# One core, linear attention beside a state-space convolution: another order, other places, banks and copy engines for the same operations

## The chip, the core and the metric

The kernel runs on one core of a Trainium2 chip. The core has a matrix engine (PE, with its weight loads PEld), a vector engine (DVE), a scalar engine (ACT), a general engine (POOL) and a sync engine (SP), which here issues nearly all transfers. Each engine takes its own instructions strictly in the order in which the program lists them; engines wait for each other through semaphores. The metric is the device time of one execution in microseconds. Three executions of the kernel before took 239.25, 239.59 and 239.7 us: median 239.59.

## The reference

Two independent blocks share the call, and their outputs are laid side by side. All inputs are bf16.

```python
# block A: linear attention, S = 2048 rows, D = 448, 16 heads of 28
qkv = x @ wqkv                              # split into q, k, v by head
phi_q = [softmax(q @ w_phi), softmax(-q @ w_phi)]
phi_k = [softmax(k @ w_phi), softmax(-k @ w_phi)]
kv, z = phi_k.T @ v, sum(phi_k)
a = (phi_q @ kv / (phi_q @ z + 1e-6)) @ wo
# block B: a diagonal state-space model, L = 2048, D = 448, N = 256 states
K[d, l] = Re( sum_n C[d,n] * dt[d] * B[d,n] * exp(dt[d] * A[d,n] * l) )
b = causal_convolution(u, K) + u * Dskip    # in the reference by FFT
out = concatenate([a, b], axis=-1)
```

## The kernel before

**The work.** Block A is done in `key_side` (eight pairs of row tiles: projections on PE, exponentials on ACT, a transposing transfer of the exponentials, sums, reciprocals and products on DVE) and in four calls of `query_side` (512 rows each). Its weights are folded first: `fold_weights` multiplies W_phi into W_q and W_k. Block B first brings A, B and C into a layout by states (`to_states`), computes powers of the complex pole (exponentials for the size, sines for the angle), and then for each of four groups of channels builds tables (`rotations`, `dampings`, `damp`, `far`, `hi_tables`), sums them on PE to the kernel K (`build_k`), scatters it through DRAM (`scatter_k`), takes its spectrum by matrix products (`kernel_spectrum`), multiplies spectra on DVE and transforms back (`conv`). The spectrum of u is made once, in `signal_spectrum(0)` and `signal_spectrum(1)`.

**The order.** Nothing is issued while the functions run. Each step calls `prog.add` and becomes an operation with a running number (0 to 1035) and an engine; one operation is a single instruction, save on PE, where it is a group of matmuls. At the end `prog.run(ORDER)` issues the operations in the order of a list of numbers. So the list alone decides in which order each engine's queue stands. Three more lists are read as the steps are recorded: `PLACES` gives each buffer its byte offset in SBUF (buffers may share a place one after the other), `SLOTS` gives each PE group its bank or pair of banks of PSUM (eight banks, 0 to 7), and `PICKS` gives each of 210 copies, scalings and squares its engine, A for ACT or V for DVE. A step that writes to a place or bank waits until the reader of what was there is done. The tile framework adds these waits.

**Operations that the text names by number.**

| number | engine | what it is (line) |
|---|---|---|
| 0, 3 | SP, ACT | load of log_dt (275); load of A_re, issued from ACT's queue (280) |
| 5, 7, 9, 6, 8 | SP | loads of A_im, B_re, B_im, C_re, C_im (285) |
| 10 to 25 | SP | 16 transposing loads of x (287), 14 to 17 the second 512 rows |
| 26, 28, 31 to 34 | SP | loads of W_qk, of most of W_V, of W_phi in four blocks (291, 293, 298) |
| 41, 42, 43 | ACT, DVE, either | exp of log_dt, DG, and DGN = -DG (305 to 309) |
| 44, 49 | PE | A_re and A_im to states (333) |
| 45 to 48, 50 to 53 | either, DVE | their copies and differences (337, 338) |
| 54 to 57 | DVE | products of C and B (342) |
| 58 to 62 | ACT | five exponentials, 128, 16, 8, 32 and 64 times the log of the pole's size (353) |
| 63, 65; 64, 66 | PE; either | the products to states (356) and their copies (357) |
| 70, 71; 74, 75; 77, 78; 80, 81; 83, 84 | ACT | cosine and sine for 128; 16; 8; 32; 64 (366, 367) |
| 72, 76, 79, 82, 85 | DVE | size times angle for 128, 16, 8, 32, 64 (368) |
| 86 to 88 | either, DVE | the square of the power 128 (372 to 374) |
| 104, 106; 105, 107; 108, 109 | PE; either; DVE | first block of u: reversal of its rows in two halves, the copies, sum and difference (411 to 415) |
| 139, 141; 140, 142; 143, 144 | PE; either; DVE | the same for the second block of u |
| 95, 116, 119, 126 | PE, either, SP, either | a transposition of weights (391), a copy of the signal's spectrum (429), a store of it (431), another such copy |
| 167, 168 | DVE | the diagonal of Dskip, in two parts (443) |
| 196 | PE | arguments of the first dampings (461) |
| 294 | PE | a key projection, on the second 512 rows of x (601) |

**The start before.** ORDER begins 3 0 41 1 2 42, so the load of A_re is the first entry of ACT's queue and the load of log_dt the first of SP's. The groups 104, 106, 139 and 65 follow each other in banks 4 and 5, 63 and 141 in 0 and 1, and 196 has 6 and 7.

## Time and profile before

| | |
|---|---|
| median of three executions | 239.59 us |
| the profiled execution | 239.25 us, span 237.4 us from first to last instruction |
| busy: PE / DVE / ACT / POOL | 210.4 / 220.2 / 186.5 / 4.9 us |
| table loads of ACT | 10, 1.28 us each |
| bytes moved | 36.40 MB, mean 153 GB/s |
| mean granted clock of PE | 0.984 |

In a line of the profile, L220 is line 220 of the kernel. As most steps go through small helpers (177 tensor-tensor on DVE, 198 activations, 205 copies, 220 groups of matmuls), the line tells the helper and not the place; shapes and times tell which step it is. "Idle before, releaser" is the time in which an engine did nothing before an instruction, and whose semaphore ended it. PE's busy time has modelled ends. The granted clock is the share of PE's clock that a throttle let through.

### The profile page before, as it was taken

What the parts mean: (1) busy time and instruction counts of PE and PEld (TensorE: products, weight loads), DVE (VectorE), ACT (ScalarE), POOL (GpSimd) and SP (SyncE); (2) the same over time, 40 slices, a digit from 0 to 9 for tenths busy, and PEclk for the clock granted to TensorE, in tenths of its full rate; (3) what the DMA queues carried; (4) which work ended last, traced back from release to release, by engine and by line L of the source; (5) the groups of instructions that cost most, each with busy time, mean ns of one, the idle gap of its engine ahead of it and who ended that gap; (6) DMA issues with size and microseconds to landing.
All of it is one profiled execution on the core that took longest, in us unless ns stands there. A gap on an engine that the chain in (4) does not pass through costs nothing. (4 is left out here: it accounts for less than half of the span.)

```text
span 237.4 us, 7131 instructions
## 1 busy us (share of the span) xinstructions
PE 210.4 (89%) x3044; PEld 152.8 (64%) x3044; DVE 220.2 (93%) x294; ACT 186.5 (79%) x324; POOL 4.9 (2%) x20
## 2 busy tenths in 40 slices
PE   1156989999998998989899999979999999999994
PEld 1143446555466665669677579755579958589993
DVE  1999999999999998989999999979999999999991
ACT  2999999999999999899999999972648545335420
POOL 2000001000000100000000000000000000000000
PEclk9995899999999999999999999999999999999999
DMA  6999944930399039989457265943689697583454
GB/s 160 243 214 260 207 113 100 275 125 3 99 213 252 7 77 175 172 155 239 128 148 161 18 124 116 277 150 95 52 254 274 134 184 240 82 178 119 70 143 98
DMA packets 81640, 36.40 MB, mean 153 GB/s; under 512 B 65480, under 2 KB 79688, under 8 KB 81224
## 3 DMA queue, kind: packets, MB, share of 16 engines
q1 hardware_dynamic: 81368, 35.71, 67.8%
q8 instruction: 24, 0.39, 0.7%
q10 hardware_dynamic: 240, 0.23, 0.3%
q14 instruction: 8, 0.07, 0.1%
HBM read 19.44 MB, written 8.62 MB: 118 GB/s over the span
## 5 line engine op out<-in xcount | busy, mean ns | idle before, releaser
L220 PE MATMUL psum<-sbuf 128*128 128x112 bf16 (+9 forms) x3000 | 208.3, 251 | 23.4 <-DVE sbuf L177 10.5
L177 DVE TENSOR_TENSOR sbuf<-sbuf 128x896 bf16<-128x896 bf16 (+13 forms) x240 | 198.9, 895 | 8.3 <-ACT sbuf L198 4.7
L220 PEld LDWEIGHTS <-sbuf 128*128 128x128 bf16 (+3 forms) x3000 | 150.2, 114 | 80.0 <-issue 18.6
L205 ACT CAST sbuf<-psum 128x448 bf16<-128x448 f32 (+4 forms) x128 | 82.2, 710 | 34.0 <-PE psum L220 33.7
L198 ACT ACTIVATE sbuf<-psum 128x448 bf16<-128x448 f32 (+4 forms) x110 | 65.6, 683 | 2.4 <-PE psum L220 2.3
L211 ACT ACTIVATE sbuf<-sbuf 128x896 bf16<-128x896 bf16 (+1 forms) x19 | 15.0, 836 | 2.8 <-DVE sbuf L177 2.7
L198 ACT ACT_TABLE_LOAD x10 | 12.8, 1283 | 1.4 <-PEq L901 1.2
L198 ACT ACTIVATE sbuf<-psum,sbuf 128x896 f32<-128x896 f32 (+3 forms) x17 | 13.5, 817 | 0.0
L208 ACT ACTIVATE sbuf<-sbuf 128x896 bf16<-128x896 bf16 (+3 forms) x11 | 9.9, 898 | 3.8 <-DVE sbuf L177 3.8
L205 ACT COPY sbuf<-psum 112x896 bf16<-112x896 bf16 (+2 forms) x12 | 7.2, 645 | 2.2 <-PE psum L230 2.2
L205 DVE CAST sbuf<-psum 128x448 bf16<-128x448 f32 (+2 forms) x9 | 6.0, 680 | 2.4 <-PE psum L220 1.3
L215 POOL MEMSET sbuf<- 128x224 bf16 (+4 forms) x15 | 4.5, 323 | 153.4 <-PE psum L220 118.7
L205 ACT COPY sbuf<-sbuf 128x224 bf16<-128x224 bf16 (+3 forms) x15 | 6.3, 453 | 0.0
L194 DVE RECIPROCAL sbuf<-psum 128x64 bf16<-128x64 f32 x8 | 4.3, 546 | 2.0 <-PE psum L220 1.4
L177 DVE TENSOR_TENSOR sbuf<-psum,sbuf 128x448 bf16<-128x448 f32 (+3 forms) x12 | 4.9, 440 | 0.0
L230 PE MATMUL psum<-sbuf 112*112 112x112 bf16 (+1 forms) x44 | 3.7, 216 | 0.2 <-ACT sbuf L198 0.2
L230 PEld LDWEIGHTS <-sbuf 112*112 112x112 bf16 (+1 forms) x44 | 3.1, 128 | 1.0 <-DVE sbuf L177 0.3
L212 DVE TENSOR_TENSOR sbuf<-sbuf 128x1792 f32<-128x1792 f32 (+1 forms) x2 | 2.6, 1318 | 0.0
L208 DVE TENSOR_SCALAR sbuf<-sbuf 128x1568 bf16<-128x1568 bf16 (+2 forms) x5 | 2.3, 456 | 0.0
L194 DVE RECIPROCAL sbuf<-sbuf 128x64 f32<-128x64 f32 x4 | 2.2, 543 | 0.0
L189 DVE SCALAR_TENSOR_TENSOR sbuf<-sbuf 128x64 f32<-128x64 f32 (+1 forms) x5 | 1.9, 389 | 0.0
L205 ACT CAST sbuf<-sbuf 128x1792 bf16<-128x1792 f32 x1 | 1.7, 1718 | 0.0
(10 smaller groups left out, 3.9 us busy)
## 6 DMA issues: line engine op xcount, KB each, us to landing
SUd<-sbuf SPq DMA_DIRECT2D x8, 448.0 KB, 4.6
sbuf<-SCd SPq DMA_DIRECT2D x16, 224.0 KB
sbuf<-SUd SPq DMA_DIRECT2D x4, 896.0 KB
sbuf<-const SPq DMA_DIRECT2D x3, 1024.0 KB
sbuf<-const SPq DMA_DIRECT2D x8, 384.0 KB, 5.0
sbuf<-in_B_u_dram SPq DMA_DIRECT2D x4, 448.0 KB, 7.5
out_dram<-sbuf SPq DMA_DIRECT2D x4, 448.0 KB, 2.8
out_dram<-sbuf SPq DMA_DIRECT2D x16, 112.0 KB, 3.1
```

What stands on the lines that cost most here:

```text
L177: prog.add("V", lambda: nc.vector.tensor_tensor(out=o, in0=a, in1=b, op=op))
L189: prog.add("V", lambda: nc.vector.scalar_tensor_tensor(out=o, in0=a, scalar=s, in1=b, op0=op0, op1=op1))
L194: nc.vector.reciprocal(o, a)
L198: prog.add("A", lambda: nc.scalar.activation(o, a, fn, **kw))
L205: either(lambda: nc.scalar.copy(o, a), lambda: nc.vector.tensor_copy(o, a))
L208: either(lambda: nc.scalar.activation(o, a, ACT.Copy, scale=s), lambda: nc.vector.tensor_scalar_mul(o, a, s))
L211: either(lambda: nc.scalar.activation(o, a, ACT.Square), lambda: nc.vector.tensor_tensor(out=o, in0=a, in1=a, op=ALU.mult))
L212: lambda: nc.vector.tensor_tensor(out=o, in0=a, in1=a, op=ALU.mult))
L215: prog.add("G", lambda: nc.gpsimd.memset(o, v))
L220: nc.tensor.matmul(o, lhsT=l, rhs=r, **kw)
L230: nc.tensor.transpose(o, i, idn)
```

## The change

The functions stay as they are, and so do all operations and their shapes. ORDER, PLACES, SLOTS and PICKS are replaced by other lists. The load of A_re (3) is still the first entry of ACT's queue and log_dt (0) the first of SP's. Then SP has 8, 5, 7, 9, 6 and PID, where it had 5, 7, 6, 9, 8 and PID. The groups 65, 106, 141 and 139 now follow each other in banks 4 and 5, and 63, 104 and 196 in banks 6 and 7. The load 28 moves from the middle of the loads of x to a place ahead of all of them. 22 of the 210 entries of PICKS differ: 43, 138, 161, 384, 429, 865, 937, 1000, 1004, 1018 and 1034 go from DVE to ACT; 208, 210, 215, 514, 625, 654, 656, 797, 828, 879 and 882 go from ACT to DVE. (1000 and 1004 are copies of the last kernel spectrum; 1018 and 1034 are copies of the last output tiles.)

```diff
 ORDER = [int(i) for i in (
-    "3 0 41 1 2 42 43 44 35 5 49 7 60 58 62 6 45 9 27 8 67 50 52 4 51 53 71 54 70 46 37 81 77 78 56 47 38 80 57 30 "
-    "65 31 48 66 61 196 33 104 105 59 72 106 40 55 201 202 107 63 199 39 36 86 88 200 87 16 139 64 140 29 79 82 18 "
-    "141 142 108 112 17 109 143 25 198 13 197 90 205 83 160 162 26 161 84 34 75 172 163 92 178 74 91 144 113 89 165 "
-    "122 85 176 76 175 125 174 155 126 207 171 177 173 179 206 10 208 209 95 123 68 180 120 19 127 20 212 156 97 96 "
-    "69 121 211 210 110 130 128 164 11 32 98 402 132 384 111 131 133 381 145 22 99 214 101 213 100 216 21 103 404 "
-    "215 15 115 403 24 217 181 14 219 182 183 116 28 405 147 12 102 146 117 185 184 148 290 73 218 118 152 187 221 "
-    "220 186 293 124 406 134 204 136 222 94 135 137 294 223 274 114 188 170 264 279 224 226 138 129 153 225 150 276 "
...
-    "789 1006 1024 1017 989 758 1025 1026 1027 754 986 1029 1011 761 987 976 977 990 1020 1021 1033 1028 1018 1030 "
-    "777 1022 973 974 1019 1034 1035 1031 1032 "
+    "1 2 67 3 0 41 42 43 8 44 5 49 60 59 7 9 35 50 58 52 51 53 61 55 70 30 57 47 6 54 71 80 4 56 48 81 65 39 63 37 "
+    "72 74 45 66 82 46 86 38 78 88 106 83 64 104 40 107 141 77 75 87 79 105 196 142 36 139 84 109 108 140 122 62 "
+    "143 120 144 123 202 199 200 172 76 90 85 92 160 121 89 201 28 198 91 15 31 197 112 210 19 161 402 179 208 180 "
+    "17 204 125 175 205 177 68 12 69 117 178 176 33 181 113 26 404 94 183 127 174 126 34 173 95 206 118 403 97 98 "
+    "10 23 207 115 130 18 116 209 182 212 132 128 184 211 13 110 131 155 73 185 214 96 213 186 32 406 215 187 147 "
+    "119 133 29 16 217 162 111 156 216 148 188 101 103 99 189 405 203 163 124 11 102 150 14 27 165 20 218 136 21 "
+    "100 151 134 407 135 138 294 164 114 304 306 137 219 408 22 384 221 296 220 297 145 146 190 264 259 171 222 149 "
+    "157 307 191 335 409 262 24 170 289 410 152 223 267 224 225 261 193 226 228 266 153 192 279 227 291 292 93 412 "
...
+    "761 966 988 1013 1015 1017 1024 973 1025 774 613 614 989 1016 1018 990 976 987 974 1026 1027 1020 1029 1033 "
+    "1019 1021 1028 1030 961 1034 1035 1022 977 1031 1032 "
 PLACES = [64 * int(i) for i in (
-    "3536 13 4 3407 3408 2404 991 959 1071 2554 3280 778 2688 2194 435 2632 2540 935 2334 2348 1169 1522 2250 2586 "
...
+    "1554 3559 801 32 2259 2323 1399 2379 2291 2411 3303 968 1431 0 2868 1119 2564 266 37 51 507 2198 2291 0 2443 "
...
 SLOTS = [[int(c) for c in i] for i in (
-    "01 23 01 45 3 2 4 01 23 45 45 23 45 67 67 01 67 23 67 0 6 23 56 45 01 45 01 01 01 45 23 01 67 01 67 4 7 2 3 1 "
...
+    "01 23 67 45 2 6 7 23 01 67 45 01 45 01 23 45 23 67 45 2 7 01 67 45 45 01 45 45 12 23 67 23 67 01 67 1 4 0 2 6 "
...
 PICKS = (
-    "VAVVVAAAAVVAAAAAAAAAAAAAAAAAAAVAAAAAAAAVAVVAAAAVVAAVAAAAAAAAAAAAAAAAAAAAAVAAAAAVAVAVAAAAAAAAAAAAAAAA"
-    "AAAAAAAAAAAAAAAAAAAAAVAAAAAAAAAAAAAAAAAAAAAAAAAAAAAAAAAAAAAAAAAAAAAAAAAVAAAAAAAAAAAAAAAAVAAAAAAAAAAA"
-    "AAVAVAVAAV"
+    "AAVVVAAAAVVAAAAAAAAAAAAAAAAAAAAAAAAAAAAAAVVAVVVVVAAVAAAAAAAAAAAAAAAAAAAAAAAAAAAVAAAVAAAAAAAAAAAVAAAA"
+    "AAAAAAAAAAAAAAAAAAAAVVAVVAAAAAAAAAAAAAAAAAAAAAAAAAAAAAAVAAAVAAAAAAAAAAAAAAAVAVAAAAAAAAAAAAAAAAAAAAAA"
+    "AAAAAAAAAA"
```

## The prediction

> **What bounds the kernel now.** I read the engines' busy times first, then the granted clock by slice, then busy time in stretches of 12 us, then the first 30 us in order of time. Busy times and clock, from the page:

> ```profile
> PE 210.4 (89%) x3044; PEld 152.8 (64%) x3044; DVE 220.2 (93%) x294; ACT 186.5 (79%) x324; POOL 4.9 (2%) x20
> ...
> PEclk9995899999999999999999999999999999999999
> ```

> DVE has 237.4 - 220.2 = 17.2 us without work, PE 27. A new order can win no more than a part of that. Busy time by stretches (length, then us busy and count of PE, PEld, DVE, ACT, POOL; then granted clock, DMA share, GB/s):

> ```profile
> 36.00:48.00 12.00, 11.76 (x99) 7.41 (x98) 11.89 (x16) 11.95 (x19) 1.16 (x3) 1.00 0.74 195
> ...
> 144.00:156.00 12.00, 10.21 (x262) 8.62 (x259) 12.00 (x17) 11.97 (x23) 0.00 (x0) 1.00 0.86 189
> ...
> 216.00:228.00 12.00, 12.00 (x249) 12.00 (x246) 11.74 (x12) 6.24 (x13) 0.00 (x0) 1.00 0.53 120
> ```

> Up to 156 us DVE and ACT are both full, later DVE and PE. A wait on any full engine is passed on to the end, unless a later wait swallows it. Most of PE's idle time lies in the first 30 us, where it waits for copies that empty its banks; PE in order of time (start, us, what, idle before it and who ended that):

> ```profile
> 11.66 3.08 PE L220 MATMUL psum<-sbuf 112*128 112x112 bf16 x23 [0.86 <-DVE sbuf L177]
> 16.32 0.54 PE L220 MATMUL psum<-sbuf 128*128 128x448 bf16 x2 [1.58 <-ACT sbuf L205]
> 19.34 3.22 PE L220 MATMUL psum<-sbuf 128*128 128x448 bf16 x20 [2.49 <-ACT sbuf L205]
> 23.15 6.21 PE L220 MATMUL psum<-sbuf 128*128 128x448 bf16 x26 [0.58 <-ACT sbuf L205]
> 29.63 0.93 PE L220 MATMUL psum<-sbuf 128*128 128x224 bf16 x8 [0.28 <-DVE sbuf L205]
> ```

> ACT and DVE in the same stretch: ACT's start-to-start time is 0.89 for a cosine (12.75 to 13.64) and 0.80 for a sine (13.64 to 14.44), it loses only 0.18 us here, and DVE loses 0.50.

> ```profile
> 12.75 1.02 ACT L198 ACTIVATE sbuf<-psum,sbuf 128x896 f32<-128x896 f32 x1
> 13.64 0.94 ACT L198 ACTIVATE sbuf<-psum 128x896 f32<-128x896 f32 x1
> 14.44 1.04 ACT L198 ACTIVATE sbuf<-psum,sbuf 128x896 f32<-128x896 f32 x1
> ...
> 24.09 0.91 ACT L205 CAST sbuf<-psum 128x896 bf16<-128x896 f32 x1 [0.18 <-PE psum L220]
> ```

> ```profile
> 25.03 3.03 DVE L177 TENSOR_TENSOR sbuf<-sbuf 128x1792 bf16<-128x1792 bf16 x2 [0.50 <-ACT sbuf L205]
> ```

> The granted clock there, in stretches of 2 us:

> ```profile
> 16.00:18.00 2.00, 0.54 (x2) 0.19 (x2) 2.00 (x3) 1.97 (x3) 0.00 (x0) 1.00 1.15 227
> 18.00:20.00 2.00, 0.66 (x2) 0.25 (x2) 2.00 (x2) 2.00 (x4) 0.00 (x0) 0.53 0.93 379
> ...
> 22.00:24.00 2.00, 1.42 (x5) 0.39 (x4) 2.00 (x3) 1.91 (x3) 0.00 (x0) 0.50 0.96 154
> 24.00:26.00 2.00, 2.00 (x9) 0.86 (x8) 1.50 (x2) 1.91 (x3) 0.00 (x0) 0.76 0.91 272
> ```

> The clock is halved from about 18.1 to 24.95. A pair of 128x448 matmuls takes 0.54 at 16.32 and 0.90 at 19.34.

> **The change, part by part.**

> *A_re.* In both kernels it is the first instruction of ACT's queue, issued at 0.80 beside the first issue of SP; PE starts at 4.49 when it lands. It is not moved: 0. The number of table loads is 10 in both: 0.

> *Engines of copies.* 22 of 210 change sides, 11 each way. DVE loses 5.5 us by its own rows (1.07 for a 128x896 cast from PSUM, five casts of 448 columns from PSUM at 0.62, five small ones at 0.17 to 0.41, 1.35 together) and gains 3.7 (two strided 128x224 copies at 0.41, four of 448 columns at 0.27, one of 224 at 0.21, one from PSUM at 0.28, squares at 0.62 and 0.38, a scale at 0.28). Two of these rows, by shape (busy, mean ns, idle before):

> ```profile
> L205 DVE CAST sbuf<-psum 128x448 bf16<-128x448 f32 x7 | 4.3, 632 | 2.3 <-PE psum L220 1.3 <-issue 1.0
> ...
> L205 DVE COPY sbuf<-sbuf 128x448 bf16<-128x448 bf16 x3 | 0.8, 269 | 0.0
> ```

> Of what it loses, 2 x 0.62 is the pair of final copies, which stood behind DVE's last product and held up nothing: on the path -5.5 + 1.24 + 3.7 = **-0.6**. The copy of 128x128 from PSUM has no row on DVE; between 0.28 (a product of that size from PSUM) and 0.62 I take 0.28, which it resembles in size; the end 0.62 costs 0.3 more. ACT loses 6.4 and gains about 5.7.

> *SP's queue at the start.* C_im now goes ahead of A_im, which lands one 224 KB load later. The first 12 us move 201 GB/s, so 1.1 us later than before at about 4.9 plus a fixed delay like A_re's: about 5.7. PE's group on A_im started at 5.60 for other reasons: +0.1.

> *Banks and order of the first 26 us.* This is the largest term. Follow it by operation numbers. DVE after 42: 50, 52, 51, 53, 55, 57, 47, 54, 56, 48 from 6.65 at about 0.56 each, ending at 12.3, as long as before. ACT: 43 first (DG is ready at 4.84, so 4.88 to 5.43), then four exponentials from 5.84 at 0.81, to 9.2; table load 1.28, to 10.5. Then, at 0.89 a cosine, 0.80 a sine and 0.68 to 0.90 a copy: 70, 71, 80, 81, 74, 45, 66 (15.45 to 16.35), 78, 83, 64 (to 18.95), 107 (to 19.75), 77, 75, 105 (21.35 to 22.3), 142 (to 23.1), 84, and ACT is free for 140 at 23.75. PE works through two pairs of banks only: 63, 104 and 196 share 6 and 7; 65, 106, 141 and 139 share 4 and 5. So 104 waits for copy 64 (19.0), 141 for 107 (19.8), and 196 for 105: 22.3. In the kernel before 196 ran at 13.04, in banks that were free. PE's queue is in order, and 139 stands behind 196. At the halved clock 196 takes 1.70 (what it took before; the same eight 128x224 matmuls take 0.93 at 29.63 at full clock) and 139 0.95: 22.3 + 1.70 + 0.95 = 24.95. So copy 140 waits 1.2 on ACT and ends at 25.9, and DVE's 143 and all behind it wait for that. DVE, by the products before it (72 at 12.35, 82, 46, 86, 88, 87, 79 to 22.6, 109, 108), is free at 24.65: it waits **1.3**. DVE's waits up to 143 are then 4.22 + 1.75 + 0.05 + 1.3 = 7.3 against 4.22 + 1.33 + 0.50 = 6.05 before: **+1.25**. ACT's are 1.25 + 1.38 + 0.76 + 0.41 + 1.2 = 5.0 against 4.6: +0.4.

> [...]

> *SP's queue from 8 to 50 us.* The load of W_V (28) now stands ahead of all transposed loads of x and reuses a place that DVE's 79 reads, so SP stands still from about 8 to 22.6; before it waited to 14.15. Behind it are 16 transposes (1.26 us of issue each), W_qk and the W_phi blocks. W_qk issues at about 29.3 and lands by 35; its user, transposition 95, waits for copy 126 at 39: hidden. The last transpose that the first key product (294) needs is behind the store 119, which waits for ACT's 116 (43): 14 issues at about 47.5 and lands 3.9 later, 51.4; 294 is due at 53: hidden by 1.5 us. If SP is later than that by x, PE loses x - 1.5.

> *The body, 26 to 220 us.* I compared running sums of the rows: work of DVE before an operation against work of ACT or PE before its source. The furthest that ACT lags behind DVE is 2.8 us in the new order (near 145 us) and 1.8 in the old; the furthest that ACT lags behind PE is 2.6 against 2.9. With ACT's +0.4 neither passes what DVE and PE had really waited by then (time less work done: 9.6 and 19.6 us). I take the same waits as before, **+0.4** for ACT's own delay, which holds up PE's banks until 156 us; the ends are -2.7 and +2.0, from the rivals.

> *The tail.* The same operations in nearly the same order: DVE's last products, then two inverse groups of PE (3.71), a copy (0.53) and the last store. 168 joins DVE's last products: +0.2, beside PE's 12.00 of 12: 0.

> Sum: +1.25 - 0.6 + 0.4 = **+1.05**. The profiled execution took 239.25, the lowest of three with a median of 239.59: 240.3 against its own time, 240.6 against the median. I forecast **240.5**.

> **Rivals.**

> *Faster: the waits of the key side go.* In the old kernel PE waits three times for the transposed exponentials, near 74, 94 and 104 us (view of the waits: us, times, longest):

> ```profile
> PE psum L220 <- DMA sbuf<-sbuf: 2.7, 3, 1.2
> ```

> In the new order the first of those transposes issues at about 64 and lands at 68, while its matmul is due at 69.6; the others come out level. If all three go, the time is 240.5 - 2.7 = 237.8. Against it: ACT is full there, so PE may wait for ACT's copies in their place. It decides for faster from 1.6 us on, all that the sum above adds and the bound of measurement.

> [...]

> *Slower: SP late for x.* Single transposes took 1.78 (at 19.18) where most took 1.26. Seven in line before 14 at +0.5 are 3.5 us, 1.5 of that is covered: 242.5. The old order had its transposes spread from 14.6 on, the new one crowds them behind 22.6.

> **How the numbers follow.** Forecast 0.44, key side 0.25, full clock 0.11, SP late 0.20. About 0.2% (0.48 us) is what a measurement can tell from no change. The forecast's own range is 239.9 to 241.6, which puts 0.03 of it within 0.2%; of the full clock's 0.11, 0.08 is within and 0.03 below. Faster 0.28, same 0.11, slower 0.61. The range reaches to both rivals: 237.6 to 243.0.

> **What the profile after would show.** The clock at a half near 18 to 25 us; a group of eight 128x224 matmuls at about 22 with a wait on ACT before it; an ACT wait on PE of about 1.2 and a DVE wait on ACT of about 1.3 near 25 us; DVE busy 218.3; SP idle from about 8 to 22.6 and no PE wait on in_A_x near 53. If DVE's 143 starts before 25.3, the head term is wrong; if PE waits for sbuf<-sbuf go, the first rival holds; a PE wait on in_A_x or in_A_wqkv speaks for the last. I would be wrong altogether if the body's waits, which I carried over unchanged, came out otherwise by more than 2 us: running sums bound them from below alone.

## The result, and the profile after

The changed kernel takes 246.51 us (median of six, 245.81 to 247.36), the kernel before 239.42 us (six runs, 238.65 to 240.12) beside it: a ratio of 1.0301, 95% interval 1.0270 to 1.0333. It is 7.1 us slower. The forecast was 240.5 us and the range ended at 243.0, so the direction was right and the size far off. The profiled execution took 246.2 us and its span is 244.5, against 237.4 before. Single runs of a kernel can come out more than 1.5% above its fastest one; the ratios and intervals here leave such runs out, the medians do not.

The page of the changed kernel, busy times, granted clock and the chain that ended last:

```profile
PE 212.8 (87%) x3044; PEld 153.4 (63%) x3044; DVE 218.3 (89%) x294; ACT 185.6 (76%) x324; POOL 6.0 (2%) x20
...
PEclk9999999999999999999999999799999999899999
...
DVE 16%; PE 11%; DMA 5%; issue 1%; SPq 1%; ACT 1%; DVEq 0%
```

DVE is busy for 218.3 us, as forecast, 1.9 less than before, and yet the span is 7.1 longer: DVE's idle time went from 17.2 to 26.2. The row of the clock has two dips, near 157 and 208 us, that before does not have. It shows none in the head, but the trace holds no record of the clock there (see the head, below). Transfers now stand in the last chain with 5%. The view of the waits of the changed kernel (engine, what waited, for what: us in total, times, longest):

```profile
PE psum L220 <- issue: 4.8, 2, 2.5
...
DVE sbuf L177 <- DMA sbuf<-SUd: 4.6, 1, 4.6
...
DVE sbuf L194 <- ACT sbuf L205: 2.8, 1, 2.8
PE psum L220 <- DMA sbuf<-sbuf: 2.3, 2, 2.2
DVE sbuf L177 <- issue: 2.3, 1, 2.3
```

and the line of the kernel before that answers to the first of these:

```profile
PE psum L220 <- issue: 2.2, 2, 1.7
```

The last of these lines is DVE's wait at 159.26, behind the first of two stops of PE that are looked at below. The 2.8 us stand ahead of the reciprocal 286, at 74.67. There the kernel before waited 0.59 us, and the changed kernel in turn no longer has four waits of 0.45 to 0.78 us that DVE had between 81 and 120 us.

**The tail.** The 4.6 us are DVE's wait ahead of operation 1012, the first product of the last group of channels. DVE, PE and SP of the changed kernel in order of time (start, us, engine, line, what, and idle before it and who ended that):

```profile
224.48 12.68 DVE L177 TENSOR_TENSOR sbuf<-sbuf 128x3584 bf16<-128x3584 bf16 x13 [4.64 <-DMA sbuf<-SUd]
```

```profile
205.82 6.42 PE L220 MATMUL psum<-sbuf 128*32 128x80 bf16 x26 [2.47 <-issue]
```

```profile
209.39 3.43 SPq L240 DMA_DIRECT2D sbuf<-KTd  x6
216.30 1.54 SPq L240 DMA_DIRECT2D out_dram<-sbuf  x3
217.94 0.47 SPq L240 DMA_DIRECT2D sbuf<-SUd  x1
```

In the kernel before, 1012 began at 219.87 without a wait and its load (1007, 896 KB) had been issued at 209.81. Now the load stands in SP's queue behind the store 777, SP stands still for 3.48 us until 216.30, and the load lands at 224.4. But 1012 also needs ScalarE's copy 996 (end 223.53, before 216.63), which hangs on PE, and 777 waits for a copy of PE's results as well. So there are two readings. Either the order of SP's queue costs 4.6 us (the queue theory), or PE is late and drags both along.

**PE's stop.** PE is late because of the stop in the second of these three views: from 203.35 to 205.82 it does nothing, in the middle of group 889, and no semaphore holds it (the page calls that "issue"). In the kernel before such a stop lasted 0.46 us in the same place. What moves meanwhile, by DMA queue, in the stretch 198.5 to 203.0 of the changed kernel:

```profile
DMA packets 1426, 1.25 MB, mean 277 GB/s; under 512 B 1257, under 2 KB 1298, under 8 KB 1426
...
q1 hardware_dynamic: 1426, 1.25, 106.6%
```

and in the stretch 203 to 205:

```profile
DMA packets 86, 0.04 MB, mean 20 GB/s; under 512 B 84, under 2 KB 84, under 8 KB 84
...
q8 instruction: 1, 0.02, 4.5%
```

The queue q8 carries instructions, 24 packets of 16 KB in each kernel. Its packet starts at 203.06, lands at 204.49, and PE goes on at 205.82. Until 203 the DMA engines were full with the load of SU[2] (962, 896 KB, issued at 197.35), a store and two transposing loads. Counting PE's matmuls and weight loads in the trace (6088 in all), the stop is at number 5042; the other stop without a semaphore, 2.34 us from 153.47, is at 3508, and a packet of q8 had started at 153.55 there as well. With the entries for semaphores in PE's queue counted too (13 ahead of the one stop, 15 ahead of the other) the numbers are 5057 and 3521, the ones that the expectations use, and they are exactly 6 times 256 apart. Both stops lie in strips of `build_k`, where a group of ten small matmuls takes 0.3 us; from 149.74 to 153.47 PE issues 70 instructions per us, so 256 last 3.7 us. The kernel before has its two stops at 3507 and 5043, which with those entries are 3521 and 5057 as well. The fetch theory: PE runs out of instructions in these strips when the packet with the next 256 stands behind other transfers. With both stops of the changed kernel comes a half clock of 3.41 us (from 155.39, just before the first one ends, and from 206.59, just behind the second), with those of before none. By sums of busy time PE lost 1.6 us more than before in the first strip, and 4.5 against 0.5 in the second.

### The profile page after: what moved, and what is told of

Its sections match the earlier page's. It is cut to its first block, busy times and chain, and to the rows that moved or that the text cites. A ratio compares the mean times of both kernels' runs of the same rounds, so it can differ in the third digit from the quotient of the medians.

```text
span 244.5 us, 7117 instructions
## 1 busy us (share of the span) xinstructions
PE 212.8 (87%) x3044; PEld 153.4 (63%) x3044; DVE 218.3 (89%) x294; ACT 185.6 (76%) x324; POOL 6.0 (2%) x20
## 3 DMA queue, kind: packets, MB, share of 16 engines
q1 hardware_dynamic: 81368, 35.71, 68.3%
HBM read 19.44 MB, written 8.62 MB: 115 GB/s over the span
## 5 line engine op out<-in xcount | busy, mean ns | idle before, releaser
L220 PE MATMUL psum<-sbuf 128*128 128x112 bf16 (+9 forms) x3000 | 210.7, 252 | 27.6 <-ACT sbuf L205 7.0
L177 DVE TENSOR_TENSOR sbuf<-sbuf 128x896 bf16<-128x896 bf16 (+12 forms) x240 | 199.1, 894 | 13.4 <-DMA sbuf<-SUd 4.6
L220 PEld LDWEIGHTS <-sbuf 128*128 128x128 bf16 (+3 forms) x3000 | 150.8, 115 | 86.0 <-issue 22.7
L205 ACT CAST sbuf<-psum 128x448 bf16<-128x448 f32 (+4 forms) x134 | 85.5, 709 | 40.9 <-PE psum L220 38.8
L198 ACT ACTIVATE sbuf<-psum 128x448 bf16<-128x448 f32 (+4 forms) x110 | 65.6, 707 | 1.0 <-PE psum L220 0.9
L211 ACT ACTIVATE sbuf<-sbuf 128x896 bf16<-128x896 bf16 (+1 forms) x17 | 13.6, 877 | 9.9 <-DVE sbuf L177 9.7
L198 ACT ACTIVATE sbuf<-psum,sbuf 128x896 f32<-128x896 f32 (+3 forms) x17 | 13.5, 817 | 0.0
L208 ACT ACTIVATE sbuf<-sbuf 128x896 bf16<-128x896 bf16 (+4 forms) x11 | 10.0, 913 | 0.8 <-DVE sbuf L299 0.8
L215 POOL MEMSET sbuf<- 128x224 bf16 (+4 forms) x15 | 5.5, 404 | 153.3 <-PE psum L220 121.4
L205 ACT COPY sbuf<-psum 112x896 bf16<-112x896 bf16 (+2 forms) x12 | 7.1, 617 | 0.0
L177 DVE TENSOR_TENSOR sbuf<-psum,sbuf 128x448 bf16<-128x448 f32 (+3 forms) x12 | 5.1, 442 | 0.3 <-ACT sbuf L205 0.2
L205 ACT COPY sbuf<-sbuf 128x224 bf16<-128x224 bf16 (+2 forms) x11 | 4.0, 374 | 0.0
L205 DVE CAST sbuf<-psum 128x448 bf16<-128x448 f32 x3 | 1.8, 645 | 2.3 <-PE psum L220 2.3
L212 DVE TENSOR_TENSOR sbuf<-sbuf 128x896 bf16<-128x896 bf16 (+2 forms) x4 | 3.6, 908 | 0.0
L205 DVE COPY sbuf<-sbuf 128x448 bf16<-128x448 bf16 (+1 forms) x10 | 2.4, 265 | 0.0
```

What stands on the lines that cost most here:

```text
L177: prog.add("V", lambda: nc.vector.tensor_tensor(out=o, in0=a, in1=b, op=op))
L198: prog.add("A", lambda: nc.scalar.activation(o, a, fn, **kw))
L205: either(lambda: nc.scalar.copy(o, a), lambda: nc.vector.tensor_copy(o, a))
L208: either(lambda: nc.scalar.activation(o, a, ACT.Copy, scale=s), lambda: nc.vector.tensor_scalar_mul(o, a, s))
L211: either(lambda: nc.scalar.activation(o, a, ACT.Square), lambda: nc.vector.tensor_tensor(out=o, in0=a, in1=a, op=ALU.mult))
L212: lambda: nc.vector.tensor_tensor(out=o, in0=a, in1=a, op=ALU.mult))
```

## Experiments

All are reorderings of the operations, or one or two more transfers; the computation is whole in each. Ratios are to runs of the kernel before on the same chip. The kernel before had a median of 240.47, 240.29, 239.93 and 240.69 us in the four batches.

**The load of SU[2] earlier.**

```diff
-    "844 812 755 908 846 617 946 875 845 758 965 848 847 849 850 1011 876 878 880 877 879 881 911 883 882 856 601 "
+    "844 812 755 908 846 617 946 962 875 845 758 965 848 847 849 850 1011 876 878 880 877 879 881 911 883 882 856 601 "
...
-    "964 891 888 889 892 754 759 1009 951 760 962 959 955 769 756 786 953 898 960 789 897 903 768 770 899 901 771 "
+    "964 891 888 889 892 754 759 1009 951 760 959 955 769 756 786 953 898 960 789 897 903 768 770 899 901 771 "
```

> The changed kernel, with the 896 KB load of SU[2] (962) issued from SP right behind 946 (about 186.3 us) instead of behind the transposing loads 964 and 1009 (197.35). Fetch theory: in the trace of after PE stops for 2.47 us at 203.35, inside a group that waits for no semaphore, because a 16 KB packet of the instruction queue q8 that should have come near 198.5 only starts at 203.06, when the load 962 and its neighbours are through; the clock is then granted by half for 3.4 us, and PE is 4.5 us behind for the rest. With the load out of the way the packet starts before 201.5, the stop is under 0.7 us, no half clock follows near 207, the store 777 and the load 1007 come about 4 us earlier, the wait of 4.6 us ahead of DVE's product 1012 shrinks to under 1 us, and the time falls by 3.5 to 4.6 us, to 242 to 243 us. Queue theory: the wait ahead of 1012 comes from SP standing still behind the store 777 (3.48 us), whatever PE does; then this edit does nothing (246 to 247 us), and the load of SU[3] still lands near 224.

Measured: 243.30 us, 1.0124 (1.0097 to 1.0151), so 1.8% of the 3.0% are gone (1.2% by the repeat of the changed kernel further down, which is 2.40% above before). PE and DVE of this kernel:

```profile
200.84 11.35 PE L220 MATMUL psum<-sbuf 128*32 128x80 bf16 x181 [1.31 <-issue]
```

```profile
221.61 12.68 DVE L177 TENSOR_TENSOR sbuf<-sbuf 128x3584 bf16<-128x3584 bf16 x13 [1.23 <-DMA sbuf<-SUd]
```

The stop at 5042 is gone and no half clock comes in this strip; 1012 waits 1.23 instead of 4.64. The load 1007 is issued at 215.30 instead of 217.94, although nothing in its own part of SP's queue was touched. The size is as the fetch theory said. Not as it said: one stop of 1.31 us is left, at number 4786, which is 256 before 5042, and there the packet had landed 3.1 us earlier (196.41).

**The load of SU[3] ahead of the stores.**

```diff
-    "775 902 900 978 957 904 776 772 991 958 954 979 980 981 999 777 605 967 968 969 1000 992 982 1003 971 1004 995 "
-    "1001 773 984 993 956 996 997 983 970 1005 602 1006 985 986 1007 1012 975 963 994 1002 972 1023 168 1014 998 "
+    "775 902 900 978 957 904 776 772 991 958 954 979 980 981 999 1007 777 605 967 968 969 1000 992 982 1003 971 1004 995 "
+    "1001 773 984 993 956 996 997 983 970 1005 602 1006 985 986 1012 975 963 994 1002 972 1023 168 1014 998 "
```

> The changed kernel, with the 896 KB load of SU[3] (1007) issued ahead of the stores 777, 605 and 602. Queue theory: the load is issued at 212.8 instead of 217.94, lands by 219.5, and DVE's product 1012 starts when DVE is free, at 219.84 instead of 224.48: 4.6 us faster, 241.9 us. Fetch theory: the product needs ScalarE's copy 996 as well, which ends only at 223.53 because PE is 4.5 us behind, so no more than 0.9 us is won: 245.6 us, and the wait is then put down to ScalarE.

Measured: 246.90 us (244.24 to 249.44), 1.0203 (1.0152 to 1.0254). The runs spread widely; the ratio lies between the two theories. The profile decides: the load is issued at 215.37, ahead of the stores, and DVE waits all the same, now for ScalarE, whose copy is late with PE:

```profile
225.51 3.96 DVE L177 TENSOR_TENSOR sbuf<-sbuf 128x3584 bf16<-128x3584 bf16 x2 [3.49 <-ACT sbuf L205]
```

```profile
207.77 4.52 PE L220 MATMUL psum<-sbuf 128*32 128x80 bf16 x16 [2.30 <-issue]
```

**Both edits.**

> The changed kernel with both edits: 962 behind 946 and 1007 ahead of 777, 605 and 602. Fetch theory: as with the first edit alone, within 0.5 us of it, since the queue then costs next to nothing; 241.7 to 242.8 us, DVE without a wait over 0.5 us between 160 and 236 us. Queue theory: as with the second edit alone, 241.9 us, with the first edit adding nothing. What is left above the kernel before (2.4 us by the traces: DVE comes to the last spectra that much later) has another cause in either case.

Measured: 243.15 us, 1.0123 (1.0100 to 1.0146): the first edit alone, to the digit. Within the interval, the order of SP's queue costs nothing once PE is on time. The queue theory falls as the main cause.

**The cause put into the kernel before.** One, and then two, stores of 1 MB to a place that nobody reads, right behind 962. (The first one adds a line above the helpers, so L220 is L221 there.)

```diff
+    SPd = dram.tile([128, 4096], BF16, name="SPd")
...
+    dma("S", SPd, GI[:, 0].rearrange("p c m x -> p (c m x)"))
...
-    "851 855 756 1008 759 768 962 769 907 605 967 959 589 771 788 953 957 908 968 978 770 955 898 958 979 772 775 "
+    "851 855 756 1008 759 768 962 1036 769 907 605 967 959 589 771 788 953 957 908 968 978 770 955 898 958 979 772 775 "
```

> The kernel before, with one more transfer: a 1 MB store of the table GI[:, 0] to a spare DRAM tile that nothing reads, issued from SP right behind the load of SU[2] (962, 194.4 us). No engine waits for it by a semaphore of its own. Fetch theory: the instruction packet that starts at 200.46 in before starts 2 to 3 us later, PE's stop of 0.46 us at 203.11 becomes 2 to 3 us, a half clock of some 3 us follows, and the time grows by 2 to 4.5 us, to 241.4 to 243.9 us. Queue theory: the traffic is free (239.2 to 240.0 us), or costs what the later KTd transfers are late by, with PE's stops as they were.

Measured: 242.34 us, 1.0064 (1.0031 to 1.0098). PE's stop at 5043 is 1.47 us instead of 0.46 and the packet starts at 202.11 instead of 200.46:

```profile
204.55 7.64 PE L221 MATMUL psum<-sbuf 128*128 128x112 bf16 x61 [1.47 <-issue]
```

Traffic that only SP issues and nobody awaits lengthens the kernel by 1.5 us by the medians; the expected 2 to 4.5 were too many, and no half clock came. The profiled run is one of the quickest of the ten (240.41 us, about the median of the kernel before), so how much of the 1.5 us its stop makes can't be read from it.

> The kernel before with two such 1 MB stores behind the load 962 instead of one (one made the packet that starts at 200.46 start at 202.11, the stop 1.47 instead of 0.46 us, and the time 0.64% longer). Fetch theory: the packet starts near 204.5, the stop is 3 to 4.5 us with a half clock behind it, and the time is 1.5 to 2.5% above before. Queue theory: the same 0.6%, or what the transfers of KTd are late by.

Measured: 243.18 us, 1.0115 (1.0064 to 1.0167). The packet starts at 203.00 (expected: 204.5) and the stop is 1.84 us (expected: 3 to 4.5), without a half clock behind it. This run does not give a dose: DVE waited 2.80 us for an ordinary store (589) that the two had made late.

```profile
209.33 10.30 DVE L178 TENSOR_TENSOR sbuf<-sbuf 128x896 bf16<-128x896 bf16 x11 [2.80 <-DMA out_dram<-sbuf]
```

**The order of the first loads, the key side, the head.** Of the next four, one starts from the kernel before and three from the kernel with both edits of the tail (1.23% above before).

```diff
-    "1 2 67 3 0 41 42 43 8 44 5 49 60 59 7 9 35 50 58 52 51 53 61 55 70 30 57 47 6 54 71 80 4 56 48 81 65 39 63 37 "
+    "1 2 67 3 0 41 42 43 44 5 49 60 59 7 9 8 35 50 58 52 51 53 61 55 70 30 57 47 6 54 71 80 4 56 48 81 65 39 63 37 "
```

> The changed kernel with the two edits of the tail (962 behind 946, 1007 ahead of 777; 1.23% above the kernel before) and, beside them, the load of C_im (8) put behind that of B_im (9), so that A_im is again the first of the six that SP loads. DVE's wait ahead of its copy 50 falls from 2.48 to 1.3 to 1.5 us and the first 60 us of DVE run 1.0 us earlier. If DVE sets the pace from there on: 1.0 us faster (0.8% above before). If ScalarE sets it until 75 us (it is busy without a gap from 12 to 70 us in after): the wait ahead of the reciprocal 286 grows from 3.1 to 4.1 us by as much, and the time stays within 0.4 us. The recorded prediction had priced this order of loads at 0.1 us.

Measured: 242.77 us, 1.0107 (1.0064 to 1.0151): not to be told from 1.0123. DVE's wait ahead of 50 fell from 2.48 to 1.64, but this run's stop at 3508 was 3.06 us against 1.87.

```diff
-    "3 0 41 1 2 42 43 44 35 5 49 7 60 58 62 6 45 9 27 8 67 50 52 4 51 53 71 54 70 46 37 81 77 78 56 47 38 80 57 30 "
+    "3 0 41 1 2 42 43 44 35 8 5 49 7 60 58 62 6 45 9 27 67 50 52 4 51 53 71 54 70 46 37 81 77 78 56 47 38 80 57 30 "
```

> The kernel before, with the load of C_im (8) issued ahead of that of A_im (5) and nothing else moved: one term of the recorded prediction by itself, priced there at 0.1 us. By the trace of after (A_im's user 49 begins 0.7 us later than in before, DVE's copy 50 at 7.24 instead of 6.50) DVE starts 0.7 to 1.0 us later; if DVE sets the pace, 0.7 to 1.0 us slower (0.3 to 0.4%); if it is taken up by a later wait, under 0.3 us.

Measured: 240.62 us, 1.0027 (1.0000 to 1.0055). DVE's copy 50 comes at 7.06 instead of 6.50, with a wait of 2.03 instead of 1.33. So this order costs about 0.65 us, with an interval from 0 to 1.3 us, and the forecast had priced it at 0.1.

```diff
-    "320 158 154 274 319 282 277 269 281 265 323 268 276 321 275 230 195 159 324 325 395 322 411 270 327 260 326 "
-    "229 328 400 194 280 413 278 284 285 290 286 283 399 398 263 293 231 414 232 397 295 329 419 401 271 309 298 "
+    "320 158 154 274 319 276 282 277 269 281 265 323 268 321 275 230 195 159 324 325 395 322 411 270 327 260 326 "
+    "229 328 400 194 280 413 278 284 285 290 283 399 398 263 293 231 414 232 397 295 329 286 419 401 271 309 298 "
```

> The changed kernel with the two edits of the tail, and on the key side ScalarE's exponential 276 ahead of 282 (four instructions earlier, so that the transposing transfer 284 is issued near 67.5 instead of 68.3 us) and DVE's reciprocal 286 behind 414 and 232. DVE's wait of 2.8 to 3.2 us near 72 to 75 us goes, or is under 0.8. If DVE's waits in the middle add up to the end: 2 to 3 us faster, 240.3 to 241.2 us (0 to 0.4% above before). If PE or the transfers after 75 us set the pace and give it back: under 1 us, and the waits further on (520 at 132, 595 at 159 us) grow by as much.

Measured: 244.46 us; its four runs lie at 240.48 and 244.31 to 244.76, too far apart for an interval. The transposing transfer 284 was issued at 67.56, against 68.30 with the tail's edits alone, and landed no earlier: its group 285 began at 74.48, against 74.33. The reciprocal 286 came at 75.09, against 74.95.

> The changed kernel with the two edits of the tail, the order of the loads, the key side's two moves, and the group 196 behind 139 on PE (so that 140 and 143 no longer wait for it). If DVE sets the pace: 1.0 us for the loads, 0.3 for 196 and 2.5 for the key side, 239.3 us, within 0.3% of the kernel before. If the middle gives it back: 241.5 to 243 us, as the kernel with the tail's edits alone.

Measured: 243.79 us, 1.0133 (1.0078 to 1.0188). With the first loads' order, 196 behind 139 and the key side's two moves, DVE's 143 starts at 24.91 instead of 26.12, without a wait, and nothing of it reaches 75 us: 286 at 75.32.

**Transposing loads out of the first strip.**

```diff
-    "705 790 714 675 719 577 640 737 677 678 545 706 575 576 800 579 715 816 739 815 707 720 738 680 546 690 791 "
+    "705 790 714 675 719 577 640 737 677 678 545 706 575 576 766 764 594 800 579 715 816 739 815 707 720 738 680 546 690 791 "
...
-    "762 686 804 742 607 860 696 766 692 581 588 683 805 711 595 687 826 764 865 583 712 594 743 943 944 697 823 "
+    "762 686 804 742 607 860 696 692 581 588 683 805 711 595 687 826 865 583 712 743 943 944 697 823 "
```

> The changed kernel with the two edits of the tail (1.23% above the kernel before) and with three transposing loads of u (766, 764, 594) issued at 141.8 us instead of 149.3 to 153.9, out of the stretch in which PE's first strip of small groups runs. Fetch theory: the instruction packet that PE asks for near 150 comes 1 to 2 us earlier than at 155.2, the stop at instruction 3521 shrinks from 2.3 to 3.4 us to 1 to 1.5, DVE's wait ahead of 595 (1.1 to 2.3 us) falls under 1: 0.5 to 1.5 us faster, 0.6 to 1.0% above the kernel before. If the middle gives it back: within 0.3 us of 1.23%.

Measured: 242.36 us, 1.0071 (1.0033 to 1.0109) over twelve runs. The packet starts at 153.87 instead of 155.16, but PE is earlier too, and the stop at 3508 is 1.74 us where it was 1.87 (expected: 1 to 1.5; the page puts this wait down to DVE, since a reciprocal ended in it):

```profile
156.52 3.92 PE L220 MATMUL psum<-sbuf 112*128 112x448 bf16 x87 [1.75 <-DVE sbuf L194]
```

The gain is half a per cent against both edits of the tail, with intervals that overlap by a little. A stop that is 0.13 us shorter doesn't make it, and DVE's wait ahead of 595 is 1.06 us as against 1.11. In the second strip, where nothing was moved, the profiles differ by more: a stop of 1.28 us at 4786 there, one of 0.86 at 5043 here. So what the gain comes from is not shown.

> The changed kernel with all of it: the tail's two edits, the three transposing loads early, A_im first, 196 behind 139, and the key side's two moves. In the kernel without the three transposing loads' move the stop near 158 took back what the head and the key side had won (DVE's waits ahead of 595 of 2.6 and 3.0 us against 1.1), so if that stop is the lid: 2 to 3 us faster than with the tail alone, 0.0 to 0.5% above the kernel before. If not: 1.0 to 1.4% above it.

Measured: 243.22 us, 1.0119 (1.0077 to 1.0160). A miss: the key side's and the head's moves, put on top, give a time 0.5% above the run before. DVE's wait moves from 286 to the reciprocal 331, ten us further on:

```profile
85.85 0.56 DVE L194 RECIPROCAL sbuf<-psum 128x64 bf16<-128x64 f32 x1 [2.92 <-ACT sbuf L198]
```

The stop at 3508 was short (1.63 us), so the lid is not that stop, as had been supposed. The waits point to 66 to 86 us, where the transfer 284 lands late and, in this run, a half clock begins at 75.10. Which of the two it is was not settled.

> The changed kernel with the tail's two edits, the three transposing loads of u early, and the load of C_im (8) behind that of B_im (9). Without the last of these: 0.71% above the kernel before. C_im first made the kernel before 0.27% slower, and alone with the tail's edits taking it back gave nothing that could be told from its interval. If the start reaches the end: 0.3 to 0.6% above before. If the transfers at 66 to 74 us set the pace in any case (DVE's reciprocal 286 came at 74.3 to 75.3 us in every version): 0.7%, as without it.

Measured: 241.43 us, 1.0039 (1.0015 to 1.0063). With the tail's edits, the transposing loads and A_im first again, 0.4% of the 3.0% is left. Beside the run with the transposing loads moved and C_im first (1.0071) the first loads are worth 0.3%, as in the kernel before; the intervals overlap.

**The changed kernel again, and PE's own order.**

> The changed kernel as it is, on the chip of the three runs beside it, as the measure for them. It was 3.0% above the kernel before (2.7 to 3.3); the same is expected, 246 to 247.5 us, with PE's stops at the instructions 3521 and 5057.

Measured: 246.22 us, 1.0240 (1.0203 to 1.0277). In this run the second strip's stop is in two pieces, 1.02 us at 4786 and 1.39 at 5042, no half clock follows, and the wait ahead of 1012 is 2.98 us, while waits near 75 and 86 us are longer. The total is steadier than its parts.

```diff
-    "964 891 888 889 892 754 759 1009 951 760 962 959 955 769 756 786 953 898 960 789 897 903 768 770 899 901 771 "
+    "964 891 759 888 889 892 754 1009 951 760 962 959 955 769 756 786 953 898 960 789 897 903 768 770 899 901 771 "
```

> The changed kernel with one move and no transfer touched: PE's group 759 (8 long matmuls, 1.7 us) ahead of 888 and 889 instead of behind them. Fetch theory: PE still runs dry at its instruction 5057 and goes on when the packet has landed, near 205.8 us, but spends 1.5 us of the stop on 759: the stop lasts 0.8 to 1.3 us instead of 2.47, the half clock behind it is rarer, and the time falls by 1 to 3 us (0.4 to 1.2%). If the stop belonged to the group 889 or to the moment, it stays at 2.3 to 2.6 us and the time stays within 0.4 us of the changed kernel's.

Measured: 245.76 us, 1.0213 (1.0168 to 1.0259): no gain that can be told. In the profiled run an earlier packet was late (it started at 197.53), so the stop came one block earlier, at 4786, exactly 256 before 5042:

```profile
200.13 3.70 PE L220 MATMUL psum<-sbuf 128*32 128x80 bf16 x99 [1.76 <-issue]
```

So the stop goes by the number of the instruction and not by the group that stands there, as the fetch theory says; that filling it with other work helps was not shown.

**Can it be taken out of the kernel before?** Four transposing loads and the load 962 moved out of its strips (594 early, 765, 763 and 966 late, 962 ahead of 1009):

```diff
-    "936 708 820 719 676 736 675 575 733 737 720 716 934 640 677 818 790 678 593 689 815 937 578 577 579 580 690 "
+    "936 708 820 719 676 736 675 575 733 737 720 716 934 640 677 818 790 678 593 689 815 937 578 577 594 579 580 690 "
...
-    "698 779 697 780 966 742 809 599 823 824 743 782 863 940 827 766 167 864 699 861 941 825 826 702 704 942 781 "
+    "698 779 697 780 765 742 809 599 823 824 743 782 863 940 827 766 167 864 699 861 941 825 826 702 704 942 781 "
...
-    "848 847 850 849 889 891 767 613 890 888 947 951 892 895 894 853 858 856 1009 852 920 854 952 893 896 857 859 "
+    "848 847 850 849 889 891 767 613 890 888 947 951 892 895 894 853 858 856 962 1009 852 920 854 952 893 896 857 859 "
```

> The kernel before, with transfers moved out of its two strips of small groups: transposing load 594 early (142 us), 763, 765 and 966 later (161 and 179 us), and the load of SU[2] (962) ahead of 1009 and 1008 (191.4 instead of 194.4 us). Fetch theory: the stop of 1.73 us at 156 shrinks below 1, that of 0.46 at 203 goes, and the kernel gets 0.5 to 1.5 us faster than before (0.2 to 0.6%). If the stops cost nothing there because DVE is the bound: within 0.2%.

Measured: 238.91 us, 0.9942 (0.9908 to 0.9976). Both old stops are under 0.3 us; a new one of 1.52 us stood at 183.57, number 4275. The second version (966 behind 1007):

> The kernel before with the transfers moved as in the version that was 0.58% faster, but the transposing load 966 issued behind 1007 (210 us) instead of at 179.5, since a new stop of 1.52 us stood at 185 there, when 966 and 763 were in flight. Fetch theory: the stop at 185 is under 0.5 us and the kernel 0.5 to 1.2% faster than before. If that stop was off the path: 0.6% as it was.

Measured: 238.36 us, 0.9915 (0.9884 to 0.9947), faster than both kernels. Its waits and its two strips:

```profile
PE psum L220 <- issue: 0.4, 2, 0.3
```

```profile
155.72 4.60 PE L220 MATMUL psum<-sbuf 128*32 128x80 bf16 x110 [0.29 <-issue]
```

```profile
202.36 9.86 PE L220 MATMUL psum<-sbuf 128*128 128x112 bf16 x106 [0.15 <-issue]
```

No operation was taken away; five transfers stand elsewhere in SP's queue.

## Why the prediction was wrong

**The step that failed is "The tail … beside PE's 12.00 of 12: 0", and with it the body's waits, "I take the same waits as before".** The body's waits were argued from running sums of DVE, ACT and PE against each other, the tail's from its nearly equal order and from PE's full 12 us. Transfers were in neither, and so neither was the supply of PE's instructions. A new order of SP's queue moved the 896 KB load 962 from 194.38 to 197.35, which is 3 us closer to 198.67, when PE begins the block of 256 instructions ahead of the stop; a packet with little in its way starts at such a moment (see the last section), and this one started at 203.06. By the runs that load's place is worth 1.2 to 1.8% (2.8 to 4.2 us: 1.0124 against 1.0240 and 1.0301), the three transposing loads in the first strip about 0.5% (1.2 us), though not by a shorter stop there. That the direction was right is luck: the terms that made the forecast slower were others. The text had named its own weak place (the body's waits coming out otherwise by more than 2 us), but the clue was in the profile of before and was not priced: PE's 2.2 us of "issue", which belong to no engine.

**The order of the first loads, "+0.1",** was mis-sized, and it is no term of its own in the sum, where at most DVE's wait of 1.75 ahead of 50 holds it. A_im one load later put DVE's 50 at 7.24 instead of 6.50 (its wait is 0.95 us longer, as 43 is no longer DVE's), and the order alone costs the kernel before 0.27% (0.65 us, with an interval from 0).

**The head, "+1.25".** DVE's 143 was put at 26.0 and came at 26.16. The sum is right and its parts are not: the wait ahead of 50 is 2.28 and not 1.75, the one ahead of 143 only 0.76 and not 1.3. ACT waited 0.86 and not 1.2. Of the changed kernel, DVE and PE in order of time, and then the stretch from 18 to 20 us (busy time and count of PE, PEld, DVE, ACT, POOL, then granted clock, DMA share, GB/s):

```profile
7.24 1.19 DVE L205 CAST sbuf<-psum 128x448 bf16<-128x448 f32 x2 [2.28 <-PE psum L220]
...
26.16 4.03 DVE L177 TENSOR_TENSOR sbuf<-sbuf 128x1792 bf16<-128x1792 bf16 x3 [0.76 <-ACT sbuf L205]
```

```profile
16.96 0.90 PE L220 MATMUL psum<-sbuf 128*128 128x448 bf16 x2 [1.33 <-ACT sbuf L205]
```

```profile
18.00:20.00 2.00, 0.53 (x2) 0.25 (x2) 2.00 (x2) 2.00 (x3) 0.00 (x0) 1.00 0.90 365
```

The 1.00 in the last line is not a clock at full speed. The trace has no record of the clock before 25.69 us, and the view counts a time without a record as full. The matmuls tell the clock themselves: the pair at 16.96 takes 0.90 us, as the pair at 19.34 of before did in its recorded half clock, against 0.54 at 16.32; and matmuls of 128x448 start 0.37 us apart up to 25.4 us, 0.19 from 25.7 us on. So the clock was at a half here, where the forecast had it, and the full clock, to which it gave a chance of 0.11, did not come; what that would have been worth no run shows. The two runs that have a record of it (half from 19.23 us with 962 earlier, from 18.99 with the key side's moves) show the same waits, ACT 0.86 and DVE 0.76. They came out shorter than forecast because ACT and DVE were later themselves: ACT was free at 24.37 and not 23.75, DVE at 25.40 and not 24.65. What of this term reaches the end no run shows: the one in which 196 was moved and 143 came at 24.91 had the loads and the key side moved too, and was no faster.

**The first rival,** that the transposed exponentials are no longer waited for, came true for the first of them (issued at 64.50 as forecast, PE's 270 without a wait) and not for the second: 284 was issued at 68.31, took 5.7 us to land, and PE waited 2.18. The waits near 94 and 104 us are gone, but with this one the sum is 2.3 against 2.7, so next to nothing was won. **Copies' engines, -0.6:** DVE's busy time of 218.3 is right to the digit; what it is worth at the end was not tested. **A_re: 0,** 10 table loads: right. **SP's queue from 8 to 50 us:** SP stood still until 23.43 (forecast 22.6), and no PE wait on x came: right.

With 962, 1007, the three transposing loads and the first loads put elsewhere (the stop at 3508 still lasts 1.90 us), the changed kernel stands 0.39% (0.15 to 0.63) above the kernel before. The forecast was 0.4% too (0.91 us). That the two agree is not to the credit of the sum: of the head term, its largest, no run shows what reaches the end. Which waits make up the 0.4% stays open.

## What to carry to other kernels

A wait of PE that a profile gives to "issue" in the middle of a group of matmuls can be the supply of instructions, as the two stops of 2.34 and 2.47 us here: see whether such stops are multiples of 256 instructions apart, look for the packet of the instruction queue that ends it, and for the large transfer ahead of that packet. In the strips of this kernel small matmuls ran at 55 to 70 instructions per us, so that 256 lasted 3.7 to 4.6 us; in such a place keep a load like 962 (896 KB, its place worth 1.2 to 1.8%) out of the 5 us before and in the strip. To change SP's order takes no operation away and adds none. And where an order is changed as a whole, sums over compute engines do not see the transfers: move the large ones against the strips by hand before saying "0".
